# Attention and two gated feed-forward blocks: scores issued by head pair, TensorE's attention work issued from a table

## Chip, cores and metric

One core of one Trainium2 chip runs the whole program. The metric is the time of one execution on the device in microseconds (us), the median of several. For this kernel a difference of about 0.2% (1.3 us) is what a measurement can tell from none. An engine is one of TensorE (PE in the profile, PEld its weight loads), VectorE (DVE), ScalarE (ACT), GpSimd (POOL) and SyncE (SP, which here only issues DMAs).

## What is computed

```python
# q, k, v: [2, 8, 576, 64] f32
scores = q @ k.T / 8 + bias          # bias[h, i, j] = relu(x[i, j] * w1 + b1) @ w2, x = log1p|i-j| / log1p(max(i, 1))
attn   = exp(scores - max); attn /= attn.sum(-1) + 1e-9
x      = (attn @ v) as [1152, 512]
h      = x @ w_in;  x = (h * clip(h + 3, 0, 6) / 6) @ w_out                    # d_ff 2048
xn     = x / rms(x) * rms_g
out    = (silu(xn @ w_gate) * (xn @ w_val)) @ w_out2                           # d_ff 1536
```

## The kernel before, in words

**Stages.** First the attention, with the bias tables built beside it, then two feed-forward parts (`unit1`/`second`, then `unit2`/`second`) that run a hand-written order. The feed-forward weights come as 64-bit words; DVE, ACT and POOL turn each into a high and a low float32r tile (`conv_turn`), a few of them already while the attention runs.

**Attention units.** The 1152 rows are cut into nine tiles of 128 rows, the seventh of which (`COMB`) holds the last 64 rows of both batches. A tile has eight heads, taken in four pairs: unit `u` is pair `u % 4` of tile `u // 4`, 36 units in all. A unit's steps are named as in the plan:

- `S` (`scores`, L427): q times k for one head, 128 x 576 scores in one of two buffers of the pool `ps_s`. TensorE does it in two row halves of 64 that run side by side, in two passes each, so that the trace has four matmuls for one head (eight for `COMB`). Before, `S` of head 0 and `S` of head 1 are two steps.
- `D` (`softmax_d`, L441, DVE): adds the bias and takes the row maximum; it frees the score buffer. `E` (`softmax_a`, L452, ACT): exp and row sum.
- `T` parts 0, 1, 2 (`e_turn`, L86): nine 128 x 128 transposes, four for each head and one across both, into three buffers of `ps_t`. `C` (`e_copy`, L472) copies each part to SBUF (`et`), on the engine that the table `ET` names.
- `PV` (`pv`, L490): 10 products with v, 20 matmuls in the trace (40 for `COMB`).
- once in a tile: `qT` (transposes of q, tile `qps`), `rb`, `rps` (transposes of 1/sum), `rt` (their copy), `xf`, `xh`, `xl`.

**Bias.** For each of 36 groups of 16 rows: `R` (`bias_R`, four tiles of 128 x up to 576, most on DVE), `B` (`bias_mm`, L357, four products into `ps_t`, or eight into `ps_s` when a row needs over 512 columns), `EV` (two copies with scale, ACT or DVE), `ST` (store to DRAM, SP). A unit's bias is read back from DRAM by `bias_load` (`bl`, SP), in the skewed form that it needs.

**Order.** Each step has a key, worked out from `PARAMS` (unit number plus an offset by kind), and is emitted by key. Up to the key `man` (-0.96) the engines run the emitted order as written (`tc.manual_schedule`); behind it a scheduler in the build puts the instructions of every engine in the order that its own timing model finds. Buffers of a pool are handed out by the same scheduler.

**Loads.** All DMAs are issued by SP in one row; k blocks go through the tag `rawk` (four buffers), each freed by the transposes `kT` of the block that it held.

Of the kernel before, what the change touches and what calls it, by code (L numbers as in the profile page):

```python
# [10 lines left out]
F32 = mybir.dt.float32  # L11
# [7 lines left out]
def shape_tables():  # L19
# [7 lines left out]


PARAMS = dict(
    g0=-5.972, gs=0.601, g8=-0.524, gt=-0.138, g14=1.055, gr=1.076, man=-0.96, zra=-0.531, zrd=-0.393, zrp=-1.107,  # L30
    zb=0.442, zev=0.711, zst=0.263, zevd=-77.57, zkt=-0.534, zkc=0.263, zqh=0.09, rd=-0.054, ra=-0.354, rp=0.346,
    b=0.242, ev=0.359, st=0.097, evd=82.888, k0=-5.351, k1=-3.46, k2=-2.983, k3=-0.198, k4=-0.333, k5=1.346,
    k6=2.486, k7=1.028, k8=2.644, lk=-2.593, cc=-5.654, kt=0.51, kc=0.179, lv0=0.001, lv1=1.464, q0=-3.292, q1=-0.28,
    q2=0.79, q3=4.828, lq1=-0.018, lq=-2.569, qa=0.311, qb=4.328, qh=0.06, bl=-3.209, s0=-0.452, s1=0.01, d0=0.245,
    d1=0.116, e0=0.934, e1=1.216, t0=1, t1=1.874, t2=1.529, c0=0.653, c1=0.389, c2=0.434, pv=2.825, ri=1.245,
    rb=1.468, rps=2.385, rt=2.634, xf=3.608, xh=4.242, xl=4.531, w=0.894, ws=0.496,
)
# [6 lines left out]
SLOTS = dict(wr=3, na=0, nb=8, ns=29)  # L44
BUFS = dict(rawk=4, rawq=2, qp=2, bp=5, ep=2, etp=3, sm=3, Rp=11, evp=4, xa=1, ps_s=2, ps_t=3, ps_v=1)


@with_exitstack
def kernel(ctx, tc, q, k, v, w1, b1, w2, w_in, w_out, w_gate, w_val, w_out2, rms_g, dtab, ntab, itab, out):
    nc = tc.nc  # L50
    B, H, S, D = q.shape
# [5 lines left out]
    SH = S // 2  # L57
# [35 lines left out]
    pend = []  # L93
# [128 lines left out]
    if True:  # L222
# [192 lines left out]

        e_t, sum_t, m_t = {}, {}, {}

        def scores(u, a):

            t, p = divmod(u, 4)  # L420
            h = 2 * p + a
            s = ps_s.tile([128, 2, 512], F32, tag="s", name="s")
            cols = [(0, slice(0, 64)), (1, slice(64, 128))] if t == COMB else [(TILES[t][0], slice(0, 128))]
            for b, sl in cols:
                for r in range(2):
                    rows = slice(64 * r, 64 * r + 64)
                    nc.tensor.matmul(  # L427
                        s[sl, r, :SH], lhsT=q_t[t][h // 4][rows, h % 4, sl], rhs=kS[b][rows, h, :], start=True, stop=True,
                    )
            if a == 0:  # L430
                e_t[u] = ep.tile([128, 2, S], F32, tag="e", name="e")
                if p == 0:
                    sum_t[t] = sm.tile([128, H], F32, tag="sum", name="sum")
                    m_t[t] = sm.tile([128, H], F32, tag="m", name="m")
            ps_of["s", u, a] = s

        def softmax_d(u, a):
            s = ps_of["s", u, a]
# [126 lines left out]
        def at(key, name, needs, fn, *args):  # L565
            plan.append((key, len(plan), name, needs, fn, args))
# [10 lines left out]
        for i, n in enumerate(n for c in order for n in range(8 * c, min(8 * c + 8, NG))):  # L577
            g = group_key(i)
            z = "z" if i < 8 else ""
            R_eng[n] = START[i] if i < 8 else MID[i % len(MID)]  # L580
# [32 lines left out]
        for u in range(NU):  # L613
# [46 lines left out]
        while x < NU + 1:  # L660
            at(x, ("w", x), [("free groups",)], weights)
            x += P["ws"]

        done = set()

        def emit(lo, hi):
            for key, _, name, needs, fn, args in sorted(plan, key=lambda z: z[:2]):
                if lo <= key < hi:
                    bad = [z for z in needs if z not in done]
                    assert not bad, (key, name, bad)  # L670
                    fn(*args)
                    done.add(name)
# [190 lines left out]
        with tc.manual_schedule():  # L863
            for i, (ph, n, f) in enumerate(units):
                weight_need(i)
                g = (unit1, unit2)[ph](n, f)
                queue.append((ph, n, f, g))
                while len(queue) > (2 if ph == 0 else 1):
                    finish(*queue.pop(0))
                if turn:  # L870
                    x = turn.pop(0)
                    norm_6(*x, norm_5(*x))
                late_step()
                while len(pend) < 3 and weight_want(i + 1 - len(queue), 8, 60 if ph == 0 else 8):
# [36 lines left out]
```

## Time and profile before

| | us |
|---|---|
| median of 3 runs (654.24 to 655.56) | 655.0 |
| the profiled execution | 659.37 |
| its span, first to last instruction | 657.6 |
| attention and bias: start to the first feed-forward matmul | 221.5 |
| feed-forward parts | 436 |
| TensorE busy | 636.8 (97%) |

The profiled execution is 4.4 us over the median; what is read from its trace is used for differences. A busy TensorE is modelled: a matmul's entry reaches from its start to its modelled end, and the next one starts before that end. What a block of matmuls costs is therefore read as the time from its first start to the first start of the next block.

### The profile page before, as it was taken

How to read it: one execution, taken by the hardware profiler on the slowest of the kernel's cores; microseconds unless marked ns; L12 is line 12 of the kernel's file. 1: busy time of each engine (PE TensorE's matmuls, PEld its weight loads, DVE VectorE, ACT ScalarE, POOL GpSimd, SP SyncE). 2: the span in 40 equal slices, each digit the busy share in tenths (PEclk: the TensorE clock that was granted, in tenths of full speed). 3: DMA queues.
4: the chain of work that ended last, by engine and by line, in shares of the span. 5: the costliest groups of instructions: out<-in, count | busy, mean ns of one | idle time of the engine just before them, and what ended most of it. 6: DMA issues, size and time to landing. Idle time of an engine off the chain costs nothing.

```text
span 657.6 us, 11000 instructions
## 1 busy us (share of the span) xinstructions
PE 636.8 (97%) x4174; PEld 527.3 (80%) x4174; DVE 473.4 (72%) x882; ACT 341.8 (52%) x673; POOL 143.9 (22%) x116
## 2 busy tenths in 40 slices
PE   4789999999999999999999999999999999999997
PEld 2246566666677899999999889999999999999996
DVE  6767899777655699888953689987867771387812
ACT  5856776767555555555533555564544431254411
POOL 1000100013111143333320023332333330033400
PEclk9979999999999999999999999999999999999998
DMA  6997967528600044343430034343443431045301
GB/s 151 287 289 198 280 183 226 151 65 203 184 1 2 6 155 130 127 128 129 129 96 1 1 101 123 129 128 97 128 136 122 129 121 40 33 151 169 97 1 49
DMA packets 74722, 80.17 MB, mean 122 GB/s; under 512 B 23980, under 2 KB 59436, under 8 KB 74668
## 3 DMA queue, kind: packets, MB, share of 16 engines
q1 hardware_dynamic: 74668, 79.46, 40.8%
q8 instruction: 33, 0.54, 0.3%
q14 instruction: 21, 0.17, 0.1%
HBM read 66.19 MB, written 13.25 MB: 121 GB/s over the span
## 4 chain that ended last, share of the span: by engine, by line
PE 90%; DVE 4%; DMA 3%; SPq 1%; issue 1%; ACT 0%; DVEq 0%
PE h L701 38%; PE ya L746 18%; PE yb L746 9%; PE pv L490 6%; PE s L427 6%; PE tps L86 6%; PE bps L357 4%; DVE e L441 1%; DMA bias<-biasd 1%; PE qps L86 1%; DMA raw<-in_moe_w_out_dram 1%; PE kps L86 1%; PE rps L86 1%; DVE R L344 1%; DVE et L472 1%
## 5 line engine op out<-in xcount | busy, mean ns | idle before, releaser
L151 POOL TENSOR_TENSOR wl<-wm,wh 128x512 fp32r<-128x512 f32 x85 | 125.6, 1479 | 302.2 <-ACT wh L122 195.3
L143 DVE SCALAR_TENSOR_TENSOR wm<-raw,wm 128x512 int32<-128x512 int32 x85 | 121.6, 1430 | 0.9
L710 ACT CAST gh<-r 128x384 fp32r<-128x384 f32 x84 | 43.2, 514 | 115.7 <-DVE r L733 68.8
L701 PE MATMUL h<-nh,wh 128*128 128x384 f32 x288 | 97.2, 338 | 0.0
L701 PE MATMUL h<-nh,wl 128*128 128x384 f32 x288 | 96.7, 336 | 0.0
L701 PE MATMUL h<-nl,wh 128*128 128x384 f32 x288 | 96.5, 335 | 0.0
L441 DVE CUSTOM_DVE_ANT_1 e<-s,bias 128x576 f32<-128x576 f32 x72 | 54.4, 757 | 32.9 <-PE tps L86 18.4
L452 ACT ACTIVATE e<-e,m 128x576 f32<-128x576 f32 x72 | 56.0, 778 | 19.7 <-DVE m L441 19.6
L733 DVE TENSOR_TENSOR r<-r,h 128x384 f32<-128x384 f32 x36 | 19.9, 553 | 63.2 <-PE h L701 63.2
L701 PE MATMUL h<-xh,wh 128*128 128x384 f32 x192 | 65.4, 341 | 0.0
L701 PE MATMUL h<-xh,wl 128*128 128x384 f32 x192 | 64.7, 337 | 0.0
L701 PE MATMUL h<-xl,wh 128*128 128x384 f32 x192 | 64.4, 336 | 0.0
L139 DVE SCALAR_TENSOR_TENSOR wm<-raw,wm 128x512 int32<-128x512 int32 x85 | 59.8, 704 | 2.8
L130 ACT ACTIVATE wm<-raw 128x512 f32<-128x512 f32 x85 | 57.3, 674 | 3.0 <-DMA raw<-in_moe_w_in_dram 1.1
L713 DVE TENSOR_TENSOR gl<-r,gh 128x384 fp32r<-128x384 f32 x84 | 46.6, 555 | 16.8 <-ACT gh L710 16.8
L86 PEld LDWEIGHTS tps<-ident,e 128*128 128x128 f32 x324 | 43.2, 201 | 18.4 <-issue 9.0
L427 PE MATMUL s<-kS,q 64*128 64x288 f32 (+1 forms) x320 | 56.6, 464 | 1.2 <-DVE m L441 1.2
L86 PE MATMUL tps<-ident,e 128*128 128x128 f32 x324 | 56.6, 300 | 0.0
L701 PEld LDWEIGHTS h<-nh,wh 128*128 128x128 f32 x288 | 54.1, 188 | 2.3 <-DVE nl L810 0.9
L344 DVE TENSOR_SCALAR R<-T,NB 128x368 f32<-128x368 f32 (+17 forms) x124 | 53.7, 483 | 2.2 <-PE bps L357 2.1
L701 PEld LDWEIGHTS h<-nl,wh 128*128 128x128 f32 x288 | 54.1, 188 | 1.4
L701 PEld LDWEIGHTS h<-nh,wl 128*128 128x128 f32 x288 | 54.0, 188 | 0.0
(102 smaller groups left out, 1082.6 us busy)
## 6 DMA issues: line engine op xcount, KB each, us to landing
raw<-in_moe_w_out_dram SPq DMA_DIRECT2D x33, 512.0 KB, 3.6
biasd<-ev SPq DMA_DIRECT2D x36, 295.5 KB, 3.9
raw<-in_moe_w_in_dram SPq DMA_DIRECT2D x18, 512.0 KB, 3.7
raw<-in_moe_w_gate_dram SPq DMA_DIRECT2D x18, 512.0 KB, 3.6
bias<-biasd SPq DMA_DIRECT2D x15, 576.0 KB, 5.3
raw<-in_moe_w_val_dram SPq DMA_DIRECT2D x16, 512.0 KB, 3.5
rawq<-in_q_dram SPq DMA_DIRECT2D x32, 128.0 KB, 3.6
bias<-biasd SPq DMA_DIRECT2D x10, 288.0 KB, 4.3
```

The costliest lines, as they stand in the source:

```text
L86: nc.tensor.transpose(out, in_, ident[:n, :n])
L130: nc.scalar.activation(out=m, in_=raw[:, :, 1].bitcast(F32), func=ACTF.Abs, scale=2.0 ** -112)
L139: nc.vector.scalar_tensor_tensor(out=m, in0=raw[:, :, 0], scalar=29, in1=m, op0=ALU.logical_shift_right, op1=ALU.bitwise_or,)
L143: nc.vector.scalar_tensor_tensor(out=m, in0=raw[:, :, 1], scalar=-0x80000000, in1=m, op0=ALU.bitwise_and, op1=ALU.bitwise_or,)
L151: nc.gpsimd.tensor_tensor(out=lo, in0=m, in1=hi, op=ALU.subtract)
L344: nc.vector.tensor_scalar(out=R, in0=src, scalar1=NB1[:, col], scalar2=None, op0=ALU.max)
L427: nc.tensor.matmul(s[sl, r, :SH], lhsT=q_t[t][h // 4][rows, h % 4, sl], rhs=kS[b][rows, h, :], start=True, stop=True,)
L441: nc.vector.tensor_tensor_reduce(out=e_t[u][:, a, :].rearrange("p (j r) -> p r j", r=2), in0=s[:, :, :SH], in1=bt[u][:, a, :].rearrange("p ...
L452: nc.scalar.activation(out=e_t[u][:, a, :], in_=e_t[u][:, a, :], func=ACTF.Exp, scale=-1.0, bias=m_t[t][:, h:h + 1], accum_out=sum_t[t][:, ...
L701: nc.tensor.matmul(ps, lhsT=w[wz][:, c * 128:(c + 1) * 128], rhs=x[xz][:, c, :], start=(i == 0), stop=(i == 11),)
L713: nc.vector.tensor_tensor(out=gl, in0=g, in1=gh, op=ALU.subtract)
L746: nc.tensor.matmul(y_t[ph, n, t], lhsT=g[gz][:, t * 128:(t + 1) * 128], rhs=w[wz], start=(f == 0 and i == 0), stop=(f == F - 1 and i == 2),)
```

## The change

`scores` now takes a unit and issues both heads one after the other, into both buffers of `ps_s`; the plan has one step `S` for each unit. A table, `ORDER`, lists all `S`, `T`, `PV`, `B`, `kT`, `qT` and `rps` steps; behind the key `man` such a step is emitted only when it is the table's next one, and TensorE alone runs its instructions as emitted. The other engines' order is still the scheduler's. Beside that: `rawk` has 3 buffers for 4, `ep` 3 for 2, `Rp` 12 for 11; `rt` is copied by ACT (`RT`), half of the part-2 copies too (`ET`); some offsets in `PARAMS` move (bias loads from `bl` -3.2 to -5.5 units ahead, v of batch 0 from 0.001 to 0.532); and the engines that compute the four `R` of a group are sorted. `SLOTS["far"]` is 8, which was written out before.

```diff
+ORDER = """
+B.8 kT.0,0,1 qT.1.0 S.1 T.0.0 B.14 T.0.2 S.2 kT.1,0,0 T.1.0 T.0.1 kT.1,0,1 B.15 T.1.2 S.3 T.1.1 T.2.0 kT.1,1,0 B.24
+kT.1,1,1 T.2.2 S.4 T.2.1 PV.0 PV.1 B.25 T.3.0 T.3.2 S.5 PV.2 qT.2.0 qT.1.1 B.26 T.3.1 T.4.0 rps.0 T.4.2 S.6 B.27 B.28
...
-ET = ["DADA", "DAAA", "DDDD"]
+ET = ["DADA", "DAAA", "DAAD"]
-RB, RT, XH, XL = "PDDP"
+RB, RT, XH, XL = "PADP"
-BUFS = dict(rawk=4, rawq=2, qp=2, bp=5, ep=2, etp=3, sm=3, Rp=11, evp=4, xa=1, ps_s=2, ps_t=3, ps_v=1)
+BUFS = dict(rawk=3, rawq=2, qp=2, bp=5, ep=3, etp=3, sm=3, Rp=12, evp=4, xa=1, ps_s=2, ps_t=3, ps_v=1)
...
-        def scores(u, a):
+        def scores(u):
...
+            for a in range(2):
+                h = 2 * p + a
+                s = ps_s.tile([128, 2, 512], F32, tag="s", name="s")
...
+                ps_of["s", u, a] = s
...
+            at(u + P["s0"], ("S", u), ks + [("qP", t, p // 2)], scores, u)
             for a in range(2):
                 x = "01"[a]
-                at(u + P["s" + x], ("S", u, a), ks + [("qP", t, p // 2)], scores, u, a)
-                at(u + P["d" + x], ("D", u, a), [("S", u, a), ("bl", u)], softmax_d, u, a)
+                at(u + P["d" + x], ("D", u, a), [("S", u), ("bl", u)], softmax_d, u, a)
...
+                    if short(name) in turn_of and (not line or short(name) != line[0]) and hi > P["man"]:
+                        continue
...
-        emit(P["man"], 100)
+        with tc.manual_schedule(engines={mybir.EngineType.PE}):
+            emit(P["man"], 100)
```

Three places in the built order. Line numbers are those of each file: L86, L427 and L490 of before are L103, L445 and L507 now.

TensorE late in the attention, units of the second last tile before, where `tps` are the transposes `T`, `s` the scores of one head in two rows, `pv` the products:

```order
L490 MATMUL pv<-et,vs_140 64x128 x8
L490 MATMUL pv<-et,v_142 64x128 x2
L86 MATMUL tps<-ident,e 128x128 x8
L427 MATMUL s<-kS_138,q_2076 128x288 x2
L86 MATMUL tps<-ident,e 128x128
```

The same place now, where one unit is three blocks:

```order
L507 MATMUL pv<-et,vs_140 64x128 x8
L507 MATMUL pv<-et,v_142 64x128 x2
L103 MATMUL tps<-ident,e 128x128 x9
L445 MATMUL s<-kS_139,q_2304 128x288 x4
L507 MATMUL pv<-et,vs_141 64x128 x8
```

The lone transpose between the two heads' scores has joined the eight, and the scores stand together. Over the whole attention, the order before has 81 unbroken groups of transposes (of e, q, k and 1/sum) and 53 now; the number of transposes, products and scores is the same.

SP at the start before, behind the last store of the first bias table (`biasd_74`); `vs_140` and `v_142` are v of batch 0, `rawk` a block of k:

```order
L413 DMA bias<-biasd_74 128x576 x2
L413 DMA bias<-biasd_74 128x2x576 x2
L387 DMA biasd_73<-ev 16x8x591 x2
L413 DMA bias<-biasd_74 128x2x576
L387 DMA biasd_73<-ev 16x8x591
L283 DMA rawk<-in_k_dram 128x4x128
L387 DMA biasd_73<-ev 16x8x591
L273 DMA rawq<-in_q_dram 128x4x64 x2
L291 DMA vs_140<-in_v_dram 128x4x128 x2
L293 DMA v_142<-in_v_dram 64x4x64
```

SP at the same place now:

```order
L430 DMA bias<-biasd_74 128x576 x2
L430 DMA bias<-biasd_74 128x2x576
L300 DMA rawk<-in_k_dram 128x4x128
L430 DMA bias<-biasd_74 128x2x576 x2
L404 DMA biasd_73<-ev 16x8x591 x3
L300 DMA rawk<-in_k_dram 128x4x128
L290 DMA rawq<-in_q_dram 128x4x64 x2
L300 DMA rawk<-in_k_dram 128x4x128
L404 DMA biasd_73<-ev 16x8x591
L308 DMA vs_140<-in_v_dram 128x4x128 x2
L310 DMA v_142<-in_v_dram 64x4x64
```

All k blocks now stand ahead of v, where the last k block stood behind v of batch 0 before; with three buffers, that last block waits for the transposes `kT.1,0,1`.

DVE now between head 1 of unit 10 and head 0 of unit 11 (`ISA e,m` is `D`, its second row reads the maximum):

```order
L458 ISA e,m<-s,bias 128x2x288
L458 ISA m 128x1
L489 COPY et<-tps 128x512
L361 TENSOR_SCALAR R<-T,NB_116 128x560 x4
L396 TENSOR_SCALAR ev<-bps,INV,cc 128x79
L536 TENSOR_TENSOR xf<-pv,rt 128x512
L396 TENSOR_SCALAR ev<-bps,INV,cc 128x63
L545 CAST xh_77<-xf 128x4x128
L361 TENSOR_SCALAR R<-T,NB_116 128x576 x3
L396 TENSOR_SCALAR ev<-bps,INV,cc 128x47
L361 TENSOR_SCALAR R<-T,NB_116 128x576 x4
L458 ISA e,m<-s,bias 128x2x288
```

DVE before, from a `D` to the next at the same bias groups:

```order
L441 ISA m 128x1
L344 TENSOR_SCALAR R<-T,NB_116 128x576 x2
L472 COPY et<-tps 128x128
L498 TENSOR_SCALAR ri<-sum 128x8
L344 TENSOR_SCALAR R<-T,NB_116 128x576
L499 RECIPROCAL ri<-ri 128x8
L379 TENSOR_SCALAR ev<-bps,INV,cc 128x47
L344 TENSOR_SCALAR R<-T,NB_116 128x576 x2
L139 SCALAR_TENSOR_TENSOR wm<-raw,wm 128x512
L441 ISA e,m<-s,bias 128x2x288
```

Eleven `R` stand in one run there now; before, five stood between two `D`, with a step of a weight's conversion (`wm`). The conversions have moved behind the bias, among the `D` of units 24 to 28.

## Rows read from the trace of the kernel before

**Rows 1.** The page: busy time, share of span and instructions of each engine.

```profile
PE 636.8 (97%) x4174; PEld 527.3 (80%) x4174; DVE 473.4 (72%) x882; ACT 341.8 (52%) x673; POOL 143.9 (22%) x116
```

**Rows 2.** By stretch: length; PE, PEld, DVE, ACT, POOL busy; granted PE clock; DMA share; GB/s.

```profile
37.00:44.00 7.00, 6.20 (x24) 4.15 (x24) 5.56 (x15) 3.74 (x8) 0.00 (x0) 0.52 0.99 312
44.00:95.00 51.00, 50.70 (x453) 31.49 (x453) 42.74 (x107) 37.05 (x77) 4.21 (x4) 0.95 0.81 225
95.00:160.00 65.00, 64.73 (x622) 41.34 (x621) 52.02 (x130) 44.97 (x90) 9.11 (x9) 0.95 0.59 158
164.00:221.60 57.60, 57.60 (x648) 42.20 (x644) 32.97 (x89) 33.69 (x74) 5.66 (x6) 0.95 0.20 56
221.60:657.60 436.00, 431.26 (x2232) 396.49 (x2232) 312.06 (x465) 196.68 (x374) 121.84 (x82) 0.95 0.32 100
```

**Rows 3.** Waits of PE from 44 to 221.5 us, all: total, times, longest.

```profile
PE s L427 <- DVE m L441: 1.2, 2, 1.1
PE bps L357 <- DVE m L441: 0.3, 1, 0.3
```

**Rows 4.** PE in order of time, one unit without bias: start, us, instructions.

```profile
194.30 1.11 PE L490 MATMUL pv<-et,vs 128*64 128x128 f32 x16
...
195.57 1.22 PE L86 MATMUL tps<-ident,e 128*128 128x128 f32 x8
196.72 0.78 PE L427 MATMUL s<-kS,q 64*128 64x288 f32 x4
197.43 0.33 PE L86 MATMUL tps<-ident,e 128*128 128x128 f32 x1
197.68 0.77 PE L427 MATMUL s<-kS,q 64*128 64x288 f32 x4
198.38 1.11 PE L490 MATMUL pv<-et,vs 128*64 128x128 f32 x16
```

**Rows 5.** The same view near the attention's end: nine transposes together.

```profile
216.16 1.33 PE L86 MATMUL tps<-ident,e 128*128 128x128 f32 x9
217.42 1.15 PE L490 MATMUL pv<-et,vs 128*64 128x128 f32 x15
```

**Rows 6.** The same view: transposes in two groups of four.

```profile
143.46 0.74 PE L86 MATMUL tps<-ident,e 128*128 128x128 f32 x4
144.13 1.04 PE L357 MATMUL bps<-R,W2b 128*32 128x480 f32 x8
145.11 0.74 PE L86 MATMUL tps<-ident,e 128*128 128x128 f32 x4
```

**Rows 7.** The same view: scores of two heads in a row.

```profile
49.36 0.76 PE L427 MATMUL s<-kS,q 64*128 64x288 f32 x4 [0.15 <-DVE m L441]
50.05 0.99 PE L490 MATMUL pv<-et,vs 128*64 128x128 f32 x13
```

**Rows 8.** The same view, PE and DVE, at the start.

```profile
36.37 0.76 DVE L441 CUSTOM_DVE_ANT_1 e<-s,bias 128x576 f32<-128x576 f32 x1 [2.87 <-DMA bias<-biasd]
37.80 1.12 PE L86 MATMUL kps<-ident,rawk 128*128 128x128 f32 x4 [2.60 <-DVE et L472]
44.84 0.33 PE L86 MATMUL tps<-ident,e 128*128 128x128 f32 x1
```

**Rows 9.** SP in order of time: first and last issue of v, batch 0.

```profile
38.53 3.03 SPq L291 DMA_DIRECT2D vs<-in_v_dram  x2
...
44.07 1.34 SPq L293 DMA_DIRECT2D v<-in_v_dram  x1
```

**Rows 10.** Groups of instructions to 222 us: count, busy us, mean ns, idle before.

```profile
L441 DVE CUSTOM_DVE_ANT_1 e<-s,bias 128x576 f32<-128x576 f32 x72 | 54.4, 757 | 32.9 <-PE tps L86 18.4 <-DMA bias<-biasd 6.0 <-PE s L427 4.2
L472 DVE COPY et<-tps 128x512 f32<-128x512 f32 x27 | 18.5, 685 | 0.2 <-PE tps L86 0.2
L344 DVE TENSOR_SCALAR R<-T,NB 128x560 f32<-128x560 f32 x7 | 4.3, 650 | 0.3 <-PE bps L357 0.3
L344 DVE TENSOR_SCALAR R<-T,NB 128x576 f32<-128x576 f32 x7 | 3.8, 564 | 0.0
```

More of the change, by code (lines that the diff above doesn't have):

```diff
@@ L34 @@
[L34 to L37 removed]
+    k6=2.548, k7=1.028, k8=2.644, lk=-2.593, cc=-5.654, kt=0.51, kc=0.179, lv0=0.532, lv1=1.209, q0=-3.292,
+    q1=-0.365, q2=0.79, q3=4.828, lq1=-0.018, lq=-2.569, qa=0.311, qb=4.328, qh=0.06, bl=-5.532, s0=-0.452, s1=0.01,
@@ L39 @@
+PV.34 T.35.1 rps.8 PV.35
+"""
 START = ["DDDD", "DDAA", "DDAD", "DDDA", "DDDD", "DDDA", "DDDA", "DDDD"]
 MID = ["DDDD", "DDDA"]
-ET = ["DADA", "DAAA", "DDDD"]
+ET = ["DADA", "DAAA", "DAAD"]
 KE = ["D", "D"]
-RB, RT, XH, XL = "PDDP"
-SLOTS = dict(wr=3, na=0, nb=8, ns=29)
-BUFS = dict(rawk=4, rawq=2, qp=2, bp=5, ep=2, etp=3, sm=3, Rp=11, evp=4, xa=1, ps_s=2, ps_t=3, ps_v=1)
+RB, RT, XH, XL = "PADP"
+SLOTS = dict(wr=3, na=0, nb=8, ns=29, far=8)
+BUFS = dict(rawk=3, rawq=2, qp=2, bp=5, ep=3, etp=3, sm=3, Rp=12, evp=4, xa=1, ps_s=2, ps_t=3, ps_v=1)
@@ L416 @@
         e_t, sum_t, m_t = {}, {}, {}
-        def scores(u, a):
+        def scores(u):
             t, p = divmod(u, 4)
-            h = 2 * p + a
-            s = ps_s.tile([128, 2, 512], F32, tag="s", name="s")
             cols = [(0, slice(0, 64)), (1, slice(64, 128))] if t == COMB else [(TILES[t][0], slice(0, 128))]
[L424 to L435, printed above, removed]
+            for a in range(2):
+                h = 2 * p + a
+                s = ps_s.tile([128, 2, 512], F32, tag="s", name="s")
+                for b, sl in cols:
+                    for r in range(2):
+                        rows = slice(64 * r, 64 * r + 64)
+                        nc.tensor.matmul(
+                            s[sl, r, :SH], lhsT=q_t[t][h // 4][rows, h % 4, sl], rhs=kS[b][rows, h, :], start=True, stop=True,
+                        )
+                ps_of["s", u, a] = s
+            e_t[u] = ep.tile([128, 2, S], F32, tag="e", name="e")
+            if p == 0:
+                sum_t[t] = sm.tile([128, H], F32, tag="sum", name="sum")
+                m_t[t] = sm.tile([128, H], F32, tag="m", name="m")
         def softmax_d(u, a):
@@ L579 @@
             z = "z" if i < 8 else ""
-            R_eng[n] = START[i] if i < 8 else MID[i % len(MID)]
+            R_eng[n] = "".join(sorted(START[i] if i < 8 else MID[i % len(MID)], key="PDA".index))
             for j, x in enumerate(sorted(range(4), key=lambda x: "PAD".index(R_eng[n][x]))):
@@ L662 @@
             x += P["ws"]
+        line = [tuple(int(y) if y.lstrip("-").isdigit() else y for y in z.split(".")) for z in ORDER.split()]
+        turn_of = {z: i for i, z in enumerate(line)}
+        short = lambda name: tuple(str(z).replace(" ", "").replace("(", "").replace(")", "") if isinstance(z, tuple) else z for z in name)
+        todo = sorted(plan, key=lambda z: z[:2])
+        assert sorted(turn_of) == sorted(short(z[2]) for z in todo if z[2][0] in ("S", "T", "PV", "B", "kT", "qT", "rps")), "table"
         done = set()
         def emit(lo, hi):
[L667 to L672, printed above, removed]
+            while True:
+                for z, (key, _, name, needs, fn, args) in enumerate(todo):
+                    if key >= hi:
+                        return
+                    if short(name) in turn_of and (not line or short(name) != line[0]) and hi > P["man"]:
+                        continue
+                    if all(y in done for y in needs):
+                        break
+                    assert hi > P["man"], (key, name, [y for y in needs if y not in done])
+                else:
+                    assert not todo, [(z[2], [y for y in z[3] if y not in done]) for z in todo[:5]] + line[:2]
+                    return
+                todo.pop(z)
+                if short(name) in turn_of:
+                    line.remove(short(name))
+                fn(*args)
+                done.add(name)
         with tc.manual_schedule():
             emit(-100, P["man"])
-        emit(P["man"], 100)
+        with tc.manual_schedule(engines={mybir.EngineType.PE}):
+            emit(P["man"], 100)
         actx.close()
@@ L873 @@
                 late_step()
-                while len(pend) < 3 and weight_want(i + 1 - len(queue), 8, 60 if ph == 0 else 8):
+                while len(pend) < 3 and weight_want(i + 1 - len(queue), 8, 60 if ph == 0 else SLOTS["far"]):
                     pass
```

18 lines of the change are left out of this document (15 added, 3 removed).

## The prediction

> **What bounds the kernel now.** I read the busy shares first: TensorE is busy 97% of the span [rows 1], the next engine 72%. A share over the whole says little, so I read the same by stretch. From 44 to 95 us TensorE is busy 50.70 of 51 us, from 95 to 160 64.73 of 65, from 164 to the end of the attention all 57.60, at a granted clock of 0.95, the upper of its two levels (2.4 GHz) [rows 2]. In the feed-forward parts it is busy 431.26 of 436 us, and nothing there is touched but where it starts. TensorE's own waits from 44 to 221.5 us are three, together 1.5 us [rows 3]. So from about 44 us the attention ends when TensorE has got through its instructions, and any change in the order can pay in three ways only: fewer microseconds for the same instructions, the 1.5 us of waits, or the first 44 us.
>
> Since a busy TensorE is modelled, the next look is at its instructions in order of time. One unit without bias work reads [rows 4]: products 194.30 to 195.57 (1.27 us), eight transposes to 196.72 (1.15), one head's scores to 197.43 (0.71), one lone transpose to 197.68 (0.25), the other head's scores to 198.38 (0.70). That is 4.08 us, block behind block. What differs is the price of a transpose: alone 0.25 us, as one of eight 0.14. Nine in a group took 216.16 to 217.42, 1.26 us [rows 5], so the ninth costs 0.11.
>
> **The change, part by part.**
>
> *Fewer groups of transposes.* The lone transpose stood between two heads' scores; with both heads issued together it joins the eight. It costs 0.11 in place of 0.25: 0.14 saved. Where a group of eight was split in fours around a bias product, a four takes 0.67 (143.46 to 144.13) [rows 6], two of them 1.34 against 1.15 for the eight: 0.19 saved where they join. The built order has 81 groups before and 53 now, the same transposes in both. 28 groups fewer at 0.14 to 0.19 is 3.9 to 5.3 us; I take 0.165, so **-4.6 us**. All of it lies on the path, since TensorE has no other gaps there.
>
> *Scores of two heads together.* Does the second half get cheaper too? The trace has one place where a head's scores follow another's: 49.36 to 50.05, 0.69 us [rows 7], as much as anywhere. There it had waited 0.15 first, so a small gain could be hidden. Bounds: at best each of 36 joins saves what a joined transpose saves, 36 x 0.14 = 5 us; at worst it costs the waits treated next. I take the row, **0**.
>
> *The new wait.* Both score buffers are now filled in one go, so the next unit's scores wait for `D` of both heads, and products and transposes of other units are queued behind. A unit now takes 1.27 + 1.26 + 1.40 = 3.93 us, and from the end of one head's scores to the start of that head's next lie 3.93 - 0.70 = 3.2 us. `D` takes 0.76 [rows 10], two of them 1.5: DVE has some 1.7 us left before TensorE waits. The place where DVE has more than that is the run of eleven `R` between unit 10 and unit 11: a copy 0.69, four `R` of 560 columns at 0.65, seven of 576 at 0.56 [rows 10], five short ones that I put at half the copy: 0.7 + 2.6 + 3.9 + 1.7 = 8.9 us. TensorE has three bias products, two units of products (2.5) and thirteen transposes in three groups (2.0) there; with the products at about 1.0 each [rows 6], under 8 us, so it waits near **+0.6 us**. The conversions among units 24 to 28 are runs of under 4 us, and there the cycle hides them. Against that, the longest wait of before (1.1 us) was one where scores waited for a `D` behind such work [rows 3]; it goes, **-1.2 us**. Bounds for all such waits: -1.5 (none left) to +4 (one of 0.6 in each of the six or seven units with a bias run).
>
> *The start.* Up to 27 us both orders are alike in what matters. Then TensorE waits for the first bias tables: the second unit's `D` starts at 36.37 on a DMA, TensorE's next work at 37.80 behind a wait of 2.60 us [rows 8], and its clock is at 0.52 from 37 to 44 us [rows 2]. `T.1.2` starts at 44.84 before. In the new order the same steps stand ahead of it (three scores, four k and q blocks, `B.14`, `B.15`), the bias tables are issued at the same place on SP with one k block less ahead of them, but `T.0.1` needs a buffer that DVE and ACT free only behind `D` and copies of unit 2. I count no change here, 0, with -3.5 (half of the 7 us at half clock given back) to +3.
>
> *v behind k on SP.* SP now issues all k blocks ahead of v, and with three buffers the last k block waits for `kT.1,0,1`, which stands just ahead of `B.15` and `T.1.2`, so at about 44 us. Everything of SP is queued behind it: v, then q. Before, v of batch 0 was issued from 38.53 to 45.4 us [rows 9] and the products ran from 50.05 [rows 7]. Now it starts some 5.5 us later, so that products could run at 55.5 if it were as slow; but the DMA share was 0.99 then [rows 2], and now SP stands idle ahead of it, so 51 is the other end. TensorE comes to `PV.0` with more done first: from `T.1.2` it has two units of scores (2.8), 21 transposes in three groups (2.9) and one bias product of under 1.0 (144.13 to 145.11 is one of 480 columns [rows 6]), 7 us, so at 52. The wait is 0 to 3.5; I take **+1.0 us**.
>
> *The rest.* The nine `rt` copies and 18 small copies that go to ACT are at most 0.69 us each [rows 10], 19 us, against some 58 us that ACT has idle from 44 us on [rows 2]: 0. If that cover failed, a copy would hold a transpose buffer and TensorE would wait by that copy. `ep`, `Rp` and the earlier bias loads only take waits away that nothing on the path shows. The first weights are loaded later, behind the last bias store; the stretch without bias, 57.6 us [rows 2], still lies between that and their use: 0.
>
> **Sum:** -4.6 + 0 + 0.6 - 1.2 + 0 + 1.0 = -4.2 us. The profiled execution took 659.37 us (span 657.6), so one like it would take 655.2. It stands 4.4 us over the median of 655.0; I carry the difference over: **650.8 us**.
>
> **The rivals.**
>
> *The start gains too.* If `D` of both heads of unit 1, now side by side, let TensorE work earlier, or the clock does not fall at 37 us, up to 3.5 us more come back, and joined scores may give a little: about 647. For it: 7 us at half clock are there to be had. Against: the first `D` still waits for the same DMA.
>
> *The fixed order gives the gain back.* DVE and ACT are ordered by the build's model, TensorE by the table; where a real `D` or copy is later than the table's slot, all of TensorE stands still, while before the scheduler had woven smaller pieces. Ten units in the bias stretch, 0.4 each: 655. For it: DVE is busy 52.02 of 65 us there [rows 2]. Against: 1.7 us of slack in a unit.
>
> *SP's queue makes it slower.* If `kT.1,0,1` ran only at 50 us (its own k block lands late, or the buffers free late), v would be issued from 50, `PV.0` would start at 58 or later, 6 us over the 52 above, and the 4.2 us would be gone; from there on each further microsecond is lost. With 3 more: 658. For it: one row of SP behind one k buffer. Against: its k block is issued ahead of the bias tables that came by 36.37.
>
> *The clock falls.* In the trace the granted clock stays at 0.95 from 44 us through groups of up to twelve transposes [rows 2]. The new order has groups of up to 17, some 2 us. Should the clock fall for one stretch like that of 37 to 44 us, half of 7 us is lost, 3.5: about 654, and 658 with two. The Trainium skill, "TensorE: Matmul & The Clock Gate", Part 4 (PE-mode transpose), says that transposes do not count as TensorE being busy as other matmuls do, and so speaks against joining them; by that rule this rival is the likelier. So far the rows do not bear it out.
>
> That the scheduler doesn't follow the table is no rival: the built order shows it.
>
> **How the numbers follow.** Forecast 0.58 (its own range 648.5 to 653), a start that gains 0.17 (about 647), gain given back 0.13 (about 655), SP's queue 0.09 (about 658), clock 0.03. A measurement of this kernel tells about 0.2%, 1.3 us, from no change. Faster by more is the first two, 0.75; within, the third, 0.13; slower, the rest, 0.12. The range has to leave out no more than 0.2: 645.5 holds the gaining start but for its tail, 655.5 most of the third case, and SP's queue stays outside.
>
> **What would show it.** Right: the first feed-forward matmul at about 217 us for 221.5; nine transposes in 1.26 us; both heads' scores in 1.39; PE waits from 45 us on under 3 us in sum; feed-forward 436 us as before. Wrong: scores together in well under 1.39 (the term at 0 was mis-sized); `D` ending waits of `s` in most units with bias (second rival); products waiting for v at about 52 us for over 3 us (third); a granted clock under 0.95 behind 45 us (fourth); a change in the feed-forward part, which none of this covers.

## The result, and the profile after

The changed kernel takes **647.06 us** (646.28 to 648.35, four runs) where the kernel before takes 655.02: 0.9869 of it, 95% interval 0.9853 to 0.9886, so 8.0 us or 1.3% faster. The forecast was 650.8, the right side and inside the range, but with half the gain. Beside the experiments both were taken again on one chip: 647.51 for 655.44, ratio 0.9873 (0.9855 to 0.9891).

The trace after is of an execution of 646.28 us, span 644.5. Busy time of its engines, which answers [rows 1]:

```profile
PE 622.3 (97%) x4174; PEld 527.5 (82%) x4174; DVE 461.5 (72%) x855; ACT 346.5 (54%) x700; POOL 144.5 (22%) x116
```

By stretch, which answers [rows 2] (length; then busy time of PE, PEld, DVE, ACT, POOL; granted clock; DMA share; GB/s):

```profile
37.00:44.00 7.00, 5.55 (x42) 3.90 (x41) 6.52 (x18) 5.89 (x14) 0.00 (x0) 1.00 1.09 307
44.00:95.00 51.00, 49.29 (x487) 32.95 (x487) 41.88 (x105) 37.52 (x83) 4.76 (x5) 1.00 0.74 199
95.00:160.00 65.00, 63.66 (x669) 45.39 (x665) 44.88 (x118) 48.90 (x107) 7.04 (x7) 1.00 0.70 182
164.00:208.40 44.40, 43.22 (x522) 34.66 (x520) 25.32 (x67) 29.60 (x69) 6.36 (x6) 1.00 0.15 51
208.40:644.50 436.10, 431.34 (x2233) 396.59 (x2232) 312.29 (x465) 196.70 (x374) 121.94 (x82) 1.00 0.32 100
```

The feed-forward part is 436.1 us, as before; it starts at 208.4 for 221.5. All of the gain lies ahead of it. Of the 13 us between the two starts, 4 to 5 are the profiled execution of before (659.37 for a median of 655.0), as e5 shows below. TensorE idles more than before: 1.71 us from 44 to 95 (0.30 in [rows 2]), 1.34 from 95 to 160 (0.27), 1.18 at the end (none).

One unit now, on TensorE's timeline, where [rows 4] has five blocks and 4.08 us:

```profile
196.74 1.33 PE L103 MATMUL tps<-ident,e 128*128 128x128 f32 x9
198.00 1.24 PE L445 MATMUL s<-kS,q 64*128 64x288 f32 x8
199.18 1.09 PE L507 MATMUL pv<-et,vs 128*64 128x128 f32 x16
200.10 0.39 PE L507 MATMUL pv<-et,v 128*64 128x128 f32 x4
200.42 1.34 PE L103 MATMUL tps<-ident,e 128*128 128x128 f32 x9
```

Nine transposes 1.26, both heads' scores 1.18, products 1.24: 3.68 us. The transposes take what [rows 5] said. The scores do not take the 1.39 forecast. One line's matmuls show why (ns, least, median and most). One head before, 196.72 to 197.43:

```profile
L427 PE MATMUL s<-kS,q x4: 422/464/507, 196.7 to 197.1; 64*128 64x288 f32 x4
```

Both heads now, 187.11 to 188.28:

```profile
L445 PE MATMUL s<-kS,q x8: 402/403/507, 187.1 to 187.9; 64*128 64x288 f32 x8
```

A head is two passes of two matmuls side by side. Only the first pass of a group takes 507 ns. From start to start, the first pass is 0.35 us, those that follow it 0.24, and the last takes 0.33 until another kind of work begins. So a group pays about 0.1 at its head and 0.1 at its end, and a second head that follows directly pays neither: 1.17 for two that take 0.69 each when apart. Transposes read the same way: the first is 0.22 from the second, the others 0.12 apart, the last 0.21 ahead of the next block.

[rows 7] seemed to say otherwise. There the second half had waited: its first pass came 0.57 us behind the last pass of the first half, TensorE had run empty, and it paid the full price again.

The Trainium skill, "TensorEngine Tiling (Array Packing)", Key Properties, says that changing the tiling mode drains TensorE. It gives no price. These rows agree with it, with about 0.2 us for a group of scores; no run here parts such a drain from other costs of a first and a last matmul.

### The profile page after: what moved, and what is told of

Read it like the earlier page. It is cut to its first block, busy times and chain, and to the rows that moved or that the text cites. A ratio compares the mean times of both kernels' runs of the same rounds, so it can differ in the third digit from the quotient of the medians.

```text
span 644.5 us, 10984 instructions
## 1 busy us (share of the span) xinstructions
PE 622.3 (97%) x4174; PEld 527.5 (82%) x4174; DVE 461.5 (72%) x855; ACT 346.5 (54%) x700; POOL 144.5 (22%) x116
## 4 chain that ended last, share of the span: by engine, by line
PE 88%; DVE 4%; ACT 3%; DMA 3%; issue 1%; SPq 0%; DVEq 0%; ACTq 0%
PE h L735 39%; PE ya L780 18%; PE yb L780 9%; PE pv L507 6%; PE tps L103 5%; PE s L445 5%; PE bps L374 3%; DVE R L361 1%; ACT e L469 1%; ACT ev L398 1%; DMA raw<-in_moe_w_in_dram 1%; DVE e L458 1%; DMA bias<-biasd 1%; PE qps L103 1%; DMA biasd<-ev 1%
## 5 line engine op out<-in xcount | busy, mean ns | idle before, releaser
L458 DVE CUSTOM_DVE_ANT_1 e<-s,bias 128x576 f32<-128x576 f32 x72 | 52.4, 757 | 10.6 <-PE s L445 8.0
L747 DVE TENSOR_TENSOR gl<-r,gh 128x384 fp32r<-128x384 f32 x84 | 46.6, 554 | 16.8 <-ACT gh L744 16.8
L103 PE MATMUL tps<-ident,e 128*128 128x128 f32 x324 | 53.1, 297 | 2.0 <-ACT et L489 1.6
L361 DVE TENSOR_SCALAR R<-T,NB 128x320 f32<-128x320 f32 (+17 forms) x124 | 50.6, 462 | 6.0 <-PE bps L374 5.7
L103 PEld LDWEIGHTS tps<-ident,e 128*128 128x128 f32 x324 | 41.5, 201 | 14.6 <-issue 7.3
L755 ACT ACTIVATE r<-h,half_c 128x384 f32<-128x384 f32 x48 | 27.7, 578 | 47.7 <-PE h L735 47.6
```

The source lines that it names most:

```text
L103: nc.tensor.transpose(out, in_, ident[:n, :n])
L361: nc.vector.tensor_scalar(out=R, in0=src, scalar1=NB1[:, col], scalar2=None, op0=ALU.max)
L458: nc.vector.tensor_tensor_reduce(out=e_t[u][:, a, :].rearrange("p (j r) -> p r j", r=2), in0=s[:, :, :SH], in1=bt[u][:, a, :].rearrange("p ...
L747: nc.vector.tensor_tensor(out=gl, in0=g, in1=gh, op=ALU.subtract)
```

## The experiments

Theory A: TensorE's time falls by about 0.2 us for every group of like work that is joined, whatever its kind; a change from one kind of group to another is called a switch. Rivals: the scores gain nothing (the forecast); the gain is the table's or the start's. Times are medians, ratios are to the kernel before on the same chip.

| run | us | ratio, 95% |
|---|---|---|
| e1 heads' scores apart again | 658.24 | 1.0037 (1.0022 to 1.0052) |
| e2 lone transpose behind the scores | 650.18 | 0.9915 (0.9900 to 0.9931) |
| e3 before, scores joined, scheduler's order | 658.71 | 1.0046 (1.0030 to 1.0062) |
| e4 changed, without the fixed order | 648.32 | 0.9885 (0.9869 to 0.9901) |
| e6 changed kernel again | 647.51 | 0.9873 (0.9855 to 0.9891) |
| e7 copies back on VectorE | 649.39 | 0.9901 (0.9886 to 0.9917) |
| e8 q blocks spread | 647.75 | 0.9884 (0.9864 to 0.9905) |
| e9 before, scores joined, plan's order | 660.40 | 1.0073 (1.0059 to 1.0086) |
| e10 before, plan's order | 660.26 | 1.0078 (1.0064 to 1.0092) |
| e11 first weight later | 648.41 | 0.9892 (0.9877 to 0.9907) |
| e12 the same, bias products moved | 646.67 | 0.9873 (0.9851 to 0.9894) |
| e13 first weight later, q blocks spread | 648.54 | 0.9904 (0.9887 to 0.9921) |
| e14 the same, bias products moved | 648.85 | 0.9900 (0.9880 to 0.9920) |
| e15 the same, one more q block | 648.63 | 0.9899 (0.9882 to 0.9916) |
| e16 weights at the end | 647.95 | 0.9889 (0.9874 to 0.9904) |
| e17 the same, bias products moved | 648.56 | 0.9899 (0.9882 to 0.9915) |
| e18 ten buffers for R | 644.93 | 0.9837 (0.9821 to 0.9853) |

**e5, before again.** No edit; one run.

> The kernel before, unchanged, for a second trace. In the trace that the forecast used TensorE's clock is at half from 37.3 to 44.1 us and the run is 4.4 us over its median. If that stretch is an accident of one execution, this trace has none, the fifth unit's scores start at about 45.3 instead of 48.8 us, the first feed-forward matmul at about 217 instead of 221.5, and behind the fifth unit's scores it takes the same 172.7 us. If the stretch belongs to the kernel, it is there again at 37 us.

```profile
26.00:30.00 4.00, 3.79 (x21) 0.99 (x20) 1.38 (x5) 3.26 (x7) 0.00 (x0) 0.57 0.83 262
37.00:44.50 7.50, 7.35 (x53) 4.61 (x51) 7.13 (x19) 6.79 (x15) 0.00 (x0) 1.00 1.14 324
```

The run took 654.78. The half clock of [rows 2] at 37 us is not there; a shorter stretch lies at 26 us instead. The fifth unit's scores start at 44.19 (48.44 in the first trace; the expectations count from the second pass, 0.35 later), the first feed-forward matmul comes at 216.9, and the way between is 172.7 us (173.1). So the 4.3 us by which the first trace came later to that point are an accident of that execution; [rows 8] and the start's bound of -3.5 were read from it.

**e6, changed again.** No edit.

> The changed kernel, unchanged, on the same chip as the next two. 0.987 of before, 647. From the fifth unit's scores to the first feed-forward matmul 162.2 us as in its first trace; what differs from run to run should be the first 46 us.

From the fifth unit's scores, at 46.91, on it takes 162.6 us, and 162.5 in its first trace. e5 and e6 are the fair pair: same chip, each with one short stretch at half clock in its start. TensorE's groups from that point to the feed-forward part, before:

```profile
L86 PE MATMUL tps<-ident,e 128*128 128x128 f32 x302 | 52.0, 297 | 0.0
L427 PE MATMUL s<-kS,q 64*128 64x288 f32 (+1 forms) x288 | 48.1, 449 | 1.5 <-DVE m L441 1.5
L490 PE MATMUL pv<-et,vs 128*64 128x128 f32 (+1 forms) x638 | 41.9, 268 | 1.2 <-DMA vs<-in_v_dram 1.2
```

and now:

```profile
L103 PE MATMUL tps<-ident,e 128*128 128x128 f32 x301 | 48.7, 296 | 0.5 <-ACT et L489 0.4 <-ACT ev L398 0.2
L507 PE MATMUL pv<-et,vs 128*64 128x128 f32 (+1 forms) x640 | 41.6, 268 | 0.3 <-ACT et L489 0.3
L445 PE MATMUL s<-kS,q 64*128 64x288 f32 (+1 forms) x288 | 39.7, 426 | 0.7 <-DVE m L458 0.7
```

Scores lose 8.4 us of busy time, transposes 3.3, products nothing. Busy time counts the modelled overlap too; from start to start, waits apart, scores go from 43.8 to 37.5 (63 groups to 32, 0.20 for each joined), transposes from 59.5 to 56.1, products from 46.6 to 46.5, bias products from 19.6 to 18.2. What TensorE waits for from 44 us on, before and now:

```profile
PE s L427 <- DVE m L441: 1.5, 3, 1.2
PE pv L490 <- DMA vs<-in_v_dram: 1.2, 2, 0.9
PE bps L357 <- DVE m L441: 0.5, 2, 0.3
```

```profile
PE qps L103 <- ACT et L489: 2.2, 2, 1.8
PE s L445 <- DVE m L458: 0.7, 1, 0.7
PE tps L103 <- ACT et L489: 0.4, 1, 0.4
...
```

3.2 us in all before and 4.6 now, from the fifth unit's scores on 3.2 and 4.3. (The 2.5 and 5.8 in the expectation of e13 are another count, behind 46 us.) Before, it waited for `D` and v; now mostly for ScalarE's `et` copies.

**e1, scores apart; e2, lone transpose moved.** In the table, in 30 units:

```diff
-... T.23.2 S.25 PV.22 ...
+... S.25.0 T.23.2 S.25.1 PV.22 ...      e1, S split as before
+... S.25 T.23.2 PV.22 ...               e2
```

> The changed kernel with the scores of the two heads apart again: in 30 of 36 units the lone transpose stands between the two halves, as before the change; in the other 6 the halves still follow each other. All else (table, buffers, copies on ScalarE) as changed. Theory A, what a switch of TensorE between forms of work costs (scores over 64 rows, transposes over 128, products over 64 columns): a half alone takes 0.70 and both together 1.17 in the trace of the changed kernel, so 0.23 per unit, and a transposes group more costs 0.165. Score groups rise from 37 to 67, transposes groups from 53 to 81: 30 x 0.23 + 28 x 0.165 = 11.5 us more, less up to 3 us of waits for ScalarE that the longer units hide: 655.5 to 658.5 us. Rival B, the scores joined gain nothing and only the transposes do (the forecast on record): 28 x 0.165 = 4.6 more, 651.5. Rival C, neither: the gain came from the table and the start, 647.

> The changed kernel with the lone transpose of 30 units moved behind the scores of both heads instead of ahead of them; the scores stay together. Transposes groups 53 to 74, score groups 37 as changed, switches between forms of work on TensorE up to the feed-forward part 148 to 169. Theory A (each group of transposes more costs 0.165, of switches 0.18): 21 x 0.165 = 3.5 to 21 x 0.18 = 3.8 more, about 650.7. Rival: a transposes group costs something only where it stands between two score halves, since the price is that of the scores; then no change, 647. Both heads' scores should still take 1.17 us.

e1 is about 11 us over the changed kernel by the ratios, what A says (11.5 less waits) and not what the forecast says (4.6). Against the first trace of the changed kernel the trace splits it: 5.1 us lie between the fifth unit's scores and the feed-forward part. There, from start to start, the scores take 5.3 more for 28 groups (0.19 each), the transposes 3.3 for 28 (0.12 each), the products 0.9 less, and 2.6 us of waits are hidden. 4 us lie in the start, with a stretch at half clock from 38 to 45 us, which A did not foresee, and 1.8 behind the first feed-forward matmul, where TensorE waits for a weight. So A's price holds for scores and is too high for transposes, and the sum is only by luck as near. e2 costs 2.7 to 3.0 us by the ratios; in its trace the transposes take 3.0 more from the fifth unit's scores on, for 23 groups (0.13 each), with the scores' price unchanged:

```profile
202.09 1.22 PE L103 MATMUL tps<-ident,e 128*128 128x128 f32 x8
203.24 1.24 PE L445 MATMUL s<-kS,q 64*128 64x288 f32 x8
204.41 0.33 PE L103 MATMUL tps<-ident,e 128*128 128x128 f32 x1
204.67 1.09 PE L507 MATMUL pv<-et,vs 128*64 128x128 f32 x16
```

Scores 1.17 as in the changed kernel; the lone transpose costs 0.26 wherever it stands.

**e3, scores joined alone; e9 and e10, the same in a fixed order, and its control.** e3 gives the kernel before the new `scores` and nothing else. e9 adds this edit, with `S` at the key of the second head; e10 has this edit alone.

```diff
-        emit(P["man"], 100)
+        with tc.manual_schedule(engines={mybir.EngineType.PE}):
+            emit(P["man"], 100)
```

> The kernel before with one edit: the scores of both heads of a pair are issued as one step of the plan; no table, all numbers, buffers and copies as before, so the scheduler orders TensorE. In the built order score groups fall from 71 to 51 (the scheduler still breaks some), transposes groups from 81 to 65, groups of products rise from 39 to 57, since it now puts a first product ahead of many scores; switches in all 217 to 198. Theory A, every switch costs about 0.18: 19 x 0.18 = 3.4 less than before, 651.6. Variant A2, only score and transposes groups cost (0.23 and 0.165): 20 x 0.23 + 16 x 0.165 = 7.2 less, 647.8. Rival B, joined scores alone gain nothing: 16 x 0.165 = 2.6, 652.4, or no gain at all because the scores now wait for both D: 655.

> The kernel before with two edits: the scores of both heads are one step of the plan (at the place of the second head's), and TensorE follows the plan's own order instead of the scheduler's. No table; buffers, copies and all numbers as before; the lone transposes stay alone. Built order: score groups 71 to 36, transposes groups 81 to 80, groups of products 39 to 36 (57 in the run with joined scores under the scheduler), switches 217 to 176. Theory A (a group of scores fewer is worth 0.21, the run under the scheduler lost it on broken groups of products at 0.4 each): 35 x 0.21 = 7.4 less than before, plus up to 3 of waits for D of both heads: 647.5 to 651. Forecast on record, joined scores gain nothing: 655. Rival, joined scores make TensorE wait for D and that is why the run under the scheduler was slow: 656 or more, with 6 us or more of waits for D.

> The control for the run above: the kernel before with TensorE in the plan's own order, scores of the two heads still apart. Score groups 72, transposes groups 82, groups of products 36, switches 215 against 217. If the fixed order as such gains nothing, 654 to 657; if it is what gains in the run above, 650 or less.

A's number missed in all three, and so did the control's range; e9 came out where its rival said, at 656 or more. e3 is slower than before, and its trace names the cause: scores came down, but the scheduler now puts the first products ahead of the scores.

```profile
197.21 0.49 PE L490 MATMUL pv<-et,vs 128*64 128x128 f32 x4
197.63 1.28 PE L428 MATMUL s<-kS,q 64*128 64x288 f32 x8
198.84 0.76 PE L490 MATMUL pv<-et,vs 128*64 128x128 f32 x9
```

```profile
L490 PE MATMUL pv<-et,vs 128*64 128x128 f32 (+1 forms) x638 | 48.3, 270 | 0.5 <-DMA vs<-in_v_dram 0.3 <-DVE xf L519 0.3
```

48.3 us of these products for 41.9 in e5. From start to start all products take 5.9 more for 18 more groups, 0.33 each, scores 1.1 less and transposes 1.9 less. e9 and e10 have unbroken products and differ in the scores alone (e10, then e9):

```profile
L427 PE MATMUL s<-kS,q 64*128 64x288 f32 (+1 forms) x288 | 48.0, 449 | 1.2 <-DVE m L441 1.2
```

```profile
L428 PE MATMUL s<-kS,q 64*128 64x288 f32 (+1 forms) x288 | 39.5, 426 | 0.0
```

8.5 us of busy time less (6.1 from start to start), as in the changed kernel, so the price does not need the table. Yet both take 660. What TensorE waits for from 47 us on in e10, then in e9:

```profile
PE bps L357 <- DVE m L441: 1.2, 2, 0.7
PE s L427 <- DVE m L441: 1.2, 1, 1.2
PE bps L357 <- ACT q L325: 0.2, 1, 0.2
```

```profile
PE bps L357 <- ACT q L325: 3.8, 2, 3.1
PE bps L357 <- DVE m L441: 3.1, 7, 0.7
PE pv L490 <- DMA vs<-in_v_dram: 2.2, 1, 2.2
```

2.6 us against 9.1. The wait for v lies ahead of the fifth unit's scores, which start 3.7 later in e9; behind them the waits are 2.6 against 6.8. The later start and these 4.2 us together take more than the 6.1 that the scores gave. In the plan's order joined scores stand ahead of bias products; seven short waits of these (0.3 to 0.7) end with a `D`, while the longest (3.1) ends with ScalarE's copy of q, and why that comes late stays open. In e6 no bias product waits for a `D`: its table puts other work between. That this order is why the changed kernel keeps the gain is argued from these waits; no run changes it alone.

**e4, table without the fixed order.** The plan is still emitted in the table's order.

```diff
-        with tc.manual_schedule(engines={mybir.EngineType.PE}):
-            emit(P["man"], 100)
+        emit(P["man"], 100)
```

> The changed kernel with the scheduler free to order TensorE; the plan is still emitted in the table's order, all else as changed. Switches in the built order 160 against 148 with the table, score groups 42 against 37, transposes groups 58 against 53. Theory A: 12 x 0.18 = 2.2 us more than the changed kernel, 649.2, less what the scheduler saves of the 4.7 us of waits that the fixed order has behind 44 us: 645 to 649. Rival, the fixed order itself is the gain: 652 or more.

0.8 to 1.0 us over the changed kernel by the ratios, less than can be told from nothing, with 160 switches for 148: the scheduler mostly follows the emitted order. The gain is in which order, not in its being fixed; fixing the kernel before to its plan's order (e10) made it 5 us slower.

**The new waits: e7, e8, e11 to e15.** In e6 the longest is at 156.74, the second of two q blocks in one group of 17 transposes. TensorE, then ScalarE:

```profile
154.34 0.60 PE L103 MATMUL qps<-ident,rawq 128*128 128x128 f32 x4
156.74 0.66 PE L103 MATMUL qps<-ident,rawq 128*128 128x128 f32 x4 [1.80 <-ACT et L489]
```

```profile
150.42 0.85 ACT L489 COPY et<-tps 128x512 f32<-128x512 f32 x2
153.49 0.69 ACT L147 ACTIVATE wm<-raw 128x512 f32<-128x512 f32 x1 [2.22 <-DMA raw<-in_moe_w_in_dram]
154.08 0.77 ACT L469 ACTIVATE e<-e,m 128x576 f32<-128x576 f32 x1
```

ScalarE stands before a weight conversion whose DMA has not landed, with the exponentials and copies that TensorE needs queued behind. Three causes were open: the copies moved to ScalarE, the two q blocks in one group, the weight.

```diff
 e7: ET = [..., "DAAD"] -> "DDDD";  RT "A" -> "D"
 e8: in ORDER qT.5.0, qT.6.0, qT.7.0, qT.8.0 moved behind T.17.0, T.21.0, T.25.0, T.29.0
 e11: scale of the first conversion = 0 * m[unit 25] + 2^-112     (a VectorE instruction more)
 e12: e11, and B.24, B.26, B.0, B.7 moved out of groups of transposes
 e13 = e11 + e8;  e14 = e13 + the bias products of e12;  e15 = e14, qT.3.0 moved behind T.9.1
```

> The changed kernel with the 9 rt copies and 18 small copies on VectorE again, as before the change; all else as changed. Theory A, ScalarE's copies come late since these 27 were put on it: the 3.7 us in which TensorE waits for ScalarE behind 44 us mostly go, VectorE has 10 us more to do in 160 and its own waits grow by under 1: 644.5. Rival B, the cover on VectorE is thinner: scores now wait for D of both heads, 0.3 in each unit with bias work, 650. Rival C, the waits come from the five transposes groups that want three buffers where two q blocks stand side by side, wherever the small copies are done: 647.

> The changed kernel with four entries of the table moved: the first q block of tiles 5, 6, 7 and 8 stands two units later, beside the transposes of another unit, so that no longer two q blocks stand in one group of 17 transposes with three buffers. Switches on TensorE stay at 148. Rival C of the run with the copies back: the waits of q blocks for et copies on ScalarE (1.29 at 155.2, 0.36 at 173.8 and shorter ones) go, 2 us less than the changed kernel, 645. If ScalarE is simply late everywhere, or SP's queue holds the later loads of q up: 647 to 648.

> The changed kernel with one instruction held back: ScalarE's first conversion of a weight block, which in both traces of the changed kernel waits 1.7 and 2.2 us at 151 us for its DMA with exponentials and et copies queued behind it, gets a factor that is computed from the maxima of unit 25 (a small VectorE instruction more), so that ScalarE comes to it one unit later. If that DMA wait is what TensorE's wait of 1.3 to 1.9 us at 155 us comes from: 1.5 to 2 us less than the changed kernel, 645.3, and the wait is gone. If ScalarE is late by its copies: 647, and the wait is there as before.

> The run above with four bias products moved in the table (24, 26, 0 and 7) from between transposes to a place where TensorE switches its form of work anyway or beside another bias product. Switches 148 to 141, transposes groups 53 to 49, bias groups 24 to 21. Theory A: 7 x 0.18 = 1.3 us less than the run above, 644. If the later bias products hold VectorE's or the stores' chain up, no gain or a loss of up to 1.

> The changed kernel with both edits that moved the wait without removing it: the first weight conversion held back to unit 25, and the first q block of tiles 5 to 8 two units later. If the waits behind 46 us (5.8 us in the second trace of the changed kernel, 2.5 before the change) come from two causes that each hide behind the other, the weight's DMA in ScalarE's queue at 155 us and the double q blocks at 155 and 174 us, both together take 2 to 3 off: 645. If ScalarE and VectorE are simply short of time among units 23 to 28, the wait moves again: 647 to 648.

> The run above with the four bias products moved as in the run with the first weight and bias: 7 switches fewer, 7 x 0.18 = 1.3 us less than the run above. 643.5 if both causes are right, 646 if the wait moves again.

> The run above with one more q block moved: the first of tile 3 stands with the transposes of unit 9 instead of those of unit 7, where TensorE waits 0.9 us at 73 us for ScalarE and VectorE with 17 transposes in a group. 0.9 less than the run above if that wait has the same cause as the one at 174 us; the same time if it is the bias evacuations that hold ScalarE there.

e7 is slower and its 1.9 us wait is still there: the copies are not the cause. e8 keeps a wait of 2.0 at 157.59, again with ScalarE before the DMA of a weight (2.4), and its trace has a stretch at half clock from 1 us behind it on. In e11 the wait at 155 us is gone, and one of 1.75 stands at 175.06; in e13 there are 1.84 at 166.18 and 1.01 at 176.18, the first again with ScalarE before the DMA of a weight (0.9). So holding one conversion back moves the wait along, and no run of e11 to e15 is faster than the changed kernel by more than the noise. Moving bias products, 7 switches fewer (A: 1.3), gave 1.2 us by the ratios in e12, with intervals that overlap, and nothing in e14: whether it helps is not shown. e15 is no better than e14.

**e16 and e17, all conversions later.** The edit of e11 with the maxima of unit 32 in place of 25; in e17 unit 30 and the bias products of e12.

> The changed kernel with the first weight conversion, and so the five that come ahead of the feed-forward part, held back behind the maxima of unit 32 instead of unit 25: ScalarE and VectorE do only attention work among units 22 to 31. If these conversions, which stand in ScalarE's queue ahead of exponentials and et copies, are what TensorE waits for behind 150 us wherever they are put, the waits from 150 to 185 us (3.3 us in the second trace of the changed kernel) fall under 1: 645, if the feed-forward part does not start late for its first weights (then up to 648). If the attention work alone is too much for ScalarE beside the double q blocks, the waits at 155 and 174 us stay: 647.

> The same with unit 30 in place of 32, and the four bias products moved (7 switches fewer, 1.3 us): 643.5 if the conversions are the cause, 646 if not.

The same place in e16:

```profile
153.95 1.04 PE L103 MATMUL qps<-ident,rawq 128*128 128x128 f32 x8
154.82 0.30 PE L103 MATMUL tps<-ident,e 128*128 128x128 f32 x1
```

17 transposes in a row without a wait: the double q blocks are not the cause, the conversions are. From 150 to 185 us TensorE waits for nothing. But nearer to the end of the attention TensorE waits for ScalarE's `et` copies again, with conversions in the same queue (0.92 at 191.85 and 2.24 at 203.37), and the time is that of the changed kernel. e17 has one such wait of 2.34 at 193.89. So the numbers named for the conversions as the cause (645 and 643.5) both missed.

**e18, the root.** When were these weights loaded? SP's issue of the first in the first trace before, and in e6:

```profile
76.17 0.50 SPq L110 DMA_DIRECT2D raw<-in_moe_w_in_dram  x1
```

```profile
147.77 0.59 SPq L127 DMA_DIRECT2D raw<-in_moe_w_in_dram  x1
```

72 us later, 6 us ahead of its use. (The 102 us in the expectation below is the fifth load of that trace, not the first; six are issued there before 111 us, and the first steps of three conversions run from 81 to 105 us.) In the built order the first load stands behind the last bias store with three buffers for `e` and twelve for `R`, and ahead of it with ten for `R`: the raw weights lie in memory that the bias work has to give back first. Which of the two larger buffers pushes it back was not tried apart.

```diff
-... sm=3, Rp=12, evp=4, ...
+... sm=3, Rp=10, evp=4, ...
```

> The changed kernel with 10 buffers for R instead of 12 (11 before the change). In the built order the first weight loads then stand on SP among the bias stores of the third table, as before the change, where the changed kernel issues them behind the last bias store (at 147 us; 102 us in the trace of before); the memory that a third e buffer and a twelfth R buffer take is what the raw weights lay in. If the late load is the root of TensorE's waits from 150 to 185 us, they fall under 1 us there; but three conversions now come to ScalarE and VectorE among the bias work at about 90 us, and R has two buffers less. 645 if the bias work has room for that, 648 or more if the waits move to 60 to 120 us.

644.93 us, 0.9837: by the ratios 2.1 to 2.4 us faster than the changed kernel, and the fastest version here. SP issues the first weight at 68.31 us, and the first steps of three conversions run from 77 to 97 us:

```profile
68.31 1.14 SPq L127 DMA_DIRECT2D raw<-in_moe_w_in_dram  x1
```

From 150 to 185 us, where TensorE waits 2.9 us in e6, it waits for nothing here:

```profile
155.97 1.23 PE L103 MATMUL tps<-ident,e 128*128 128x128 f32 x8
157.03 1.04 PE L103 MATMUL qps<-ident,rawq 128*128 128x128 f32 x8
```

## Why the prediction was half right

- **Fewer groups of transposes, -4.6:** right in its mechanism, a little too large. Nine take 1.26, and e1 and e2 price a group at 0.12 to 0.13 (0.14 to 0.19 forecast): 28 groups are about 3.5 us.
- **Scores of two heads together, 0 (bounds 0 to -5): this is the step that failed.** 1.17 for two of 0.69 is 0.21 a unit; 34 groups fewer are 7 us, outside the bounds, and 31 of them gave 6.3 from e5 to e6. The row taken for the price was the one half in the trace that had waited and so paid its entry twice; the prediction saw the wait of 0.15 and gave it too little weight. The bound was borrowed from transposes, which pay less.
- **The DVE run of eleven R, +0.6:** right, 0.7 at the place named. The old wait of 1.1 went, as forecast.
- **The start, 0:** the fifth unit's scores come at 46.91 in e6, 44.19 in e5, but one bias product (0.8) and five transposes (0.6) more are done by then: about +1.3, in its bounds.
- **v behind k, +1.0:** wrong in sign. SP issued the last k block at 37.06, right behind k transposes that TensorE began at 36.38, and v from 39.79, not 44; `PV.0` at 47.70 waits for nothing, and e5's waits for v (1.2) are gone. [rows 7] had been read late too: in that trace the first two products start at 48.08, not 50.05.
- **The rest, 0: the second step that failed, by about +3** (2.9 us of waits from 150 to 185 us in e6; e18 gives 2.1 to 2.4 back). The copies were weighed, and e7 says rightly so. "The first weights are loaded later" was put at 0 because 57.6 us lay ahead of their use by TensorE. But ScalarE uses them some 56 us earlier (at 153.49 in e6, the feed-forward part begins at 209.47), in a queue that TensorE waits for.
- **Feed-forward part, clock:** 436.1, and 1.00 in every stretch of the table above. The rule that spoke against joined transposes ("TensorE: Matmul & The Clock Gate", Part 4, of the Trainium skill) is not borne out by the changed kernel: groups of 17 ran at 1.00 in both its traces. But e8 and e11 show half clock behind a group of transposes with a wait inside it (last section), and no run parts the wait from the transposes.

In sum, from e5 to e6 and start to start behind the fifth unit's scores: scores -6.3, transposes -3.4, bias products -1.4, products -0.1, waits +1.1, so -10.1; ahead of them +2.7, of which 1.4 is work that has moved there from behind. The feed-forward part starts 7.4 earlier. The forecast came as near as it did because two errors went against each other: scores at 0 for -7, late weights at 0 for +3. Of the rivals the gaining start named the right time (647), mainly for a reason that is not the one found: it let joined scores give a little, but counted on the start, and e5 and e6 show that the start did not gain. The rival of the fixed order giving back took place in part, through loads and not through VectorE.

## What to carry to other kernels

Read a block's price only where it did not wait, and look at its first and last matmul apart from the rest: joining two groups saves an entry and an exit. When a buffer grows, look at what loads it pushes back, and at every engine whose queue uses them, not only at the last user. And joining work on the busiest engine pays only as long as other work is put where its buffers come free: e9 has the same 8.5 us of the scores' busy time less than e10 and keeps none of it.

## What was not expected of the hardware

- A group of fp32 scores costs TensorE about 0.2 us beyond its matmuls (0.21), a group of transposes 0.12 to 0.13 (e1, e2); breaking a group of products in two cost 0.33 (e3).
- The first trace of before reads a granted clock of 0.95 wherever it is not at half, all later ones 1.00, and the feed-forward part takes 431.35 us from its first to its last matmul in the one and 431.36 in e5: the difference in the record moves nothing.
- A stretch at half clock can follow a wait of TensorE. In e11, behind the wait of 1.75 us at 175.06 (length, busy times, clock):

```profile
172.90:175.90 3.00, 1.25 (x11) 0.83 (x9) 1.49 (x3) 2.99 (x8) 0.94 (x2) 1.00 0.33 128
175.90:179.30 3.40, 3.40 (x34) 2.37 (x36) 1.82 (x5) 1.91 (x5) 0.00 (x0) 0.51 0.51 152
```

e8 has such a stretch from 158.6 to 162.0, behind its wait of 1.99, and e9 from 85.9 to 89.3, behind one of 3.09. e6 has none behind its wait of 1.80. In the first 50 us many traces have such a stretch, each at another time, and some none (the changed kernel's first); what decides it stays open.
